# One more buffer for dK, paid for by a shared ring, in a fused two-block attention backward

## The chip, the cores and the metric

The kernel runs on one core of one Trainium2 chip. The metric is the device time of one execution in microseconds (us); less is better.

Engine names as in the profile: PE is TensorE's matmul, PEld its weight load, ACT is ScalarE, DVE is VectorE, POOL is GpSimd, SP is SyncE, whose queue issues the transfers.

## The reference

Two blocks A and B of multi-head attention over a given cache, forward and backward, all in bfloat16. Cut to what matters:

```python
# B=8, Sq=96, D=640, H=32, Sk=512, Dh=128, for block A and for block B
q = (x @ wq).reshape(B, Sq, H, Dh).transpose(0, 2, 1, 3)
p = softmax(einsum("bhqd,bhkd->bhqk", q, k_cache) * Dh ** -0.5)
o = einsum("bhqk,bhkd->bhqd", p, v_cache)
out = o.transpose(0, 2, 1, 3).reshape(B, Sq, H * Dh) @ wo
# result: concat([out_A, out_B], -1), and by jax.vjp the gradients
# dx, dk_cache, dv_cache, dwq, dwo of both blocks for a given grad_out
```

The gradients of the caches are as large as the caches: each of K, V, dK and dV is 8 x 32 x 512 x 128 elements per block, 33.6 MB. So a large part of the work is moving data.

## The kernel before

The kernel walks through block A, then block B, in pairs of heads (`HP = 2`) and, within a pair of heads, over the 8 batches. One (pair of heads, batch) is called a pair here and counted from 0, 128 in each block; pair 128 is the first of block B. A list of functions with a time tick and a slot is sorted and run once; this fixes the order in which each engine gets its instructions. A tick is one (head, batch), so a pair is two ticks. `OFF` says at which tick, relative to the pair, each stage stands:

```python
OFF = dict(kt=-3, vt=2, vn=1, kn=4, dv=7, dk=10, s2=3, s3=3, s4=4, s5=5, s6=6, s7=8, s8=9)
# kt: K transposed by the DMA   vt: V transposed by the DMA   vn, kn: V, K as they are
# dv, dk: stores of the gradients       s2...s8: the compute stages
```

Each pair has six transfers of 256 KB. All go through SyncE, and `sp` ties them into one fixed order: KT, V, store of dV, VT, K, store of dK.

```python
    def p_ldT(h, b, which):            # KT_p, VT_p: DMA transposes
            t_ = kvp.tile([128, F4 * KC, 16], BF16, name=key + "_p", bufs=5 if which == 0 else 4)
            sp(nc.sync.dma_start_transpose(t_[:], src))
# ... (cut)
    def p_ldn(h, b, which):            # K_sb, V_sb: plain loads
            t_ = kvp.tile([128, HP, KC, 128], BF16, name=key, bufs=4)
            sp(nc.sync.dma_start(t_[:].rearrange("p h c d -> p h (c d)"), src.rearrange("h (p c) d -> p h (c d)", c=KC)))
# ... (cut)
    def p_st(h, b, which):             # stores of dV_sb, dK_sb
            sp(nc.sync.dma_start(dst.rearrange("h (p c) d -> p h (c d)", c=KC), t_[:]))
```

`bufs=n` makes a ring of n tiles under one name: the next tile is to be had when the oldest of the n is no longer in use. A store that waits for its tile, or a load that waits for a free buffer, holds all that stand behind it on SyncE. The stages that the argument touches:

```python
    def c_s7(h, b):                    # dK of one head, written by ACT into half a tile
            for c in range(KC):
                nc.tensor.matmul(dK_ps[:, c * 128:(c + 1) * 128], dS_sb[:, c * 128:(c + 1) * 128], ...)
            if j == 0:
                st["dK_p"] = wk.tile([128, HP, KC * 128], BF16, name="dK_sb", bufs=3)
            nc.scalar.activation(dK_p[:, j], dK_ps[:], ACT.Identity, scale=1.0)
# ... (cut)
    # who reads the loads on PE:  V_sb in c_s45 (optp_ps), VT_p in c_s6 (dP_ps), K_sb in c_s78 (dq_dst_ps)
# ... (cut)
    def pA_wq(h):                      # wq of two heads
            wq_p = hd.tile([128, DC, HP * 128], BF16, name="wq_p", bufs=2)
    def qD(h, c_lo, c_hi):             # dwq of two heads, the same shape
                pr["dwq_sb"] = hd.tile([128, DC, HP * 128], BF16, name="dwq_sb", bufs=1)
    def qB(h, di):                     # dwo of one head goes through the ring "ob"
                st["dwo_sb"] = wk.tile([128, D], BF16, name="ob", bufs=4)
    def setup_stage(t):                # grad_out of block B, staged in the same ring "ob"
            S[("g_nat", t)] = wk.tile([128, D], BF16, name="ob", bufs=4)
# ... (cut)
            em.add(c0t + max(hk["qB"]) + 2, SL_LOAD + 0.3, qB_st(h))     # the store of dwo
```

Of the kernel before, what the change touches and what calls it, by code (L numbers as in the profile page):

```python
# [11 lines left out]
BF16 = mybir.dt.bfloat16  # L12
# [18 lines left out]
SL_LOAD = 0  # L31
# [13 lines left out]
HP = 2  # L45
# [32 lines left out]
def build_block(tc, em, tick0, blk, x, kc, vc, wq, wo, g_all, out_all, dx, dk, dv, dwq, dwo, ident, ones, pools, HG=4, first=True, groups=None):  # L78
    nc = tc.nc
    B, Sq, D = x.shape  # L80
    _, H, Sk, Dh = kc.shape
# [4 lines left out]
    DC = D // 128  # L86
    KC = Sk // 128
# [28 lines left out]
    const, ps, kvp, wk, hd, hst, grp = (pools[k] for k in ("const", "ps", "kvp", "wk", "hd", "hst", "grp"))  # L116

    def bank(shape, dt, name):
        return ps.tile(shape, dt, name=name, tag="bank")
# [48 lines left out]
    def evac(eng, dst, src, sc=None):  # L168
        if eng == "act":
            nc.scalar.activation(dst, src, ACT.Identity, scale=(1.0 if sc is None else sc))  # L170
        else:
            if sc is None:
                nc.vector.tensor_copy(dst, src)
            else:
                nc.vector.tensor_scalar(dst, src, float(sc), None, op0=ALU.mult)
# [19 lines left out]
    def pA_wq(h):  # L195
        def f():
            wq_p = hd.tile([128, DC, HP * 128], BF16, name="wq_p", bufs=2)
            with nc.allow_non_contiguous_dma(reason="per-pair wq slice"):
                sp(nc.sync.dma_start(wq_p[:], wq_v[:, :, h * 128:(h + HP) * 128]))
            for j in range(HP):  # L200
                HS[(blk, h + j)] = dict(wq_h=wq_p[:, :, j * 128:(j + 1) * 128])
        return f

    def pA(h):
        def f():
            g, hh = h // HG, h % HG
            if hh == 0:
                G[g] = dict(wo_r=grp.tile([128, HG, D], BF16, name="wo_r", bufs=2))
            wo_h = G[g]["wo_r"][:, hh]
            sp(nc.sync.dma_start(wo_h, wo[h * 128:(h + 1) * 128, :]))  # L210
            HS[(blk, h)]["wo_h"] = wo_h
            st = HS[(blk, h)]
        return f
# [86 lines left out]
    def h_alloc(h):  # L300
        def f():
            st = HS[(blk, h)]
            st["OT_h"] = hst.tile([128, T], BF16, name="OT_h", bufs=6)
            st["dQT_h"] = hst.tile([128, T], BF16, name="dQT_h")
        return f
# [140 lines left out]
    def c_s7(h, b):  # L446
        def f():
            st = CS[(blk, h, b)]
            hs = HS[(blk, h)]
            dS_sb = st["dS_sb"]  # L450
            dK_ps = bank([128, KC * 128], F32, "dK_ps")
            for c in range(KC):
                nc.tensor.matmul(dK_ps[:, c * 128:(c + 1) * 128], dS_sb[:, c * 128:(c + 1) * 128], hs["Qnat_h"][:, b * 128:(b + 1) * 128], start=True, stop=True)  # L453
            j = h % HP
            if j == 0:
                st["dK_p"] = wk.tile([128, HP, KC * 128], BF16, name="dK_sb", bufs=3)
            dK_p = CS[(blk, h - j, b)]["dK_p"]
            nc.scalar.activation(dK_p[:, j], dK_ps[:], ACT.Identity, scale=1.0)  # L458
        return f
# [35 lines left out]
    def qB_st(h):  # L495
        def f():
            sp(nc.sync.dma_start(dwo[h * 128:(h + 1) * 128, :], HS[(blk, h)]["dwo_sb"][:]))
        return f

    def qD(h, c_lo, c_hi):  # L500
        def f():
            pr = HS[(blk, h)]
            dQnat = pr["dQnat"]
            if "dwq_sb" not in pr:
                pr["dwq_sb"] = hd.tile([128, DC, HP * 128], BF16, name="dwq_sb", bufs=1)
            n = c_hi - c_lo
            w_ps = bank([128, 2, HP * 128], F32, "dwq_ps")
            for ci in range(n):
                c = c_lo + ci
                for t in range(TT):  # L510
                    nc.tensor.matmul(w_ps[:, ci, :], S["x_nat"][:, t, c * 128:(c + 1) * 128], dQnat[:, t, :], start=(t == 0), stop=(t == TT - 1))  # L511
            evac(EV["qD"], pr["dwq_sb"][:, c_lo:c_hi, :], w_ps[:, 0:n, :])
        return f
# [44 lines left out]
    for g in range(NG):  # L558
        h0 = GH0[g]
        for hh in range(groups[g]):  # L560
            h = h0 + hh
            j = h % HP
            c0t = tick0 + (h - j) * B
            hk = (HKE if first and h >= H - HP else HK if h >= HP else HK1 if first else HK2)[j]
            early = first and h < HP
            soon = 2 if first and HP <= h < 2 * HP and j == 0 else 0
            if j == 0:
                em.add(tick0 - 15 if early else c0t + hk["pA"] + soon, SL_LOAD + (1 if early else 0), pA_wq(h))
            em.add(tick0 + GT0 if early else c0t + hk["pA"] + soon, SL_LOAD - 1 if early else SL_LOAD, pA(h))
            em.add(c0t + hk["pB"], SL_HEAD, pB(h))  # L570
            em.add(c0t + OFF["s5"], SL_LOAD, h_alloc(h))
            for si in range(NTS):
                em.add(c0t + hk["pC0"][min(si, len(hk["pC0"]) - 1)], SL_HEAD, pC(h, 0, si))
                em.add(c0t + hk["pC1"][min(si, len(hk["pC1"]) - 1)], SL_HEAD, pC(h, 1, si))
            em.add(c0t + hk["pD1"], SL_HEAD, pD(h, 1))
            em.add(c0t + hk["pD0"], SL_HEAD, pD(h, 0))
            for b in range(B):
                ct = c0t + b * HP + j
                if j == 0:
                    em.add(tick0 - 13 if early and b == 0 else ct + (max(OFF["kt"], -1) if early else OFF["kt"]), SLOTS["LOAD"], p_ldT(h, b, 0))  # L580
                    em.add(ct + OFF["vt"], SLOTS["LOAD"], p_ldT(h, b, 1))
                    em.add(ct + OFF["vn"], SLOTS["LOAD"] + 0.1, p_ldn(h, b, 1))
                    em.add(ct + OFF["kn"], SLOTS["LOAD"] + 0.1, p_ldn(h, b, 0))
                    em.add(ct + OFF["dv"], SLOTS["LOAD"] + 0.2, p_st(h, b, 1))
                    em.add(ct + OFF["dk"], SLOTS["LOAD"] + 0.2, p_st(h, b, 0))
                em.add(ct + OFF["s2"], SLOTS["S2A"], c_s2a(h, b))
                em.add(ct + OFF["s2"], SLOTS["S2B"], c_s2b(h, b))
                em.add(ct + OFF["s3"], SLOTS["S3A"], c_s3a(h, b))
                em.add(ct + OFF["s3"], SLOTS["S3B"], c_s3b(h, b))
                em.add(ct + OFF["s5"], SLOTS["S5B"], c_s5b(h, b))  # L590
                em.add(ct + OFF["s4"], SLOTS["S4"], c_s4(h, b))
                S45.setdefault(ct + OFF["s5"], [None, None, None])[0] = (blk, h, b)
                S45.setdefault(ct + OFF["s4"], [None, None, None])[1] = (blk, h, b)
                S45.setdefault(ct + OFF["s6"], [None, None, None])[2] = (blk, h, b)
                S78.setdefault(ct + OFF["s8"], [None, None])[0] = (blk, h, b)
                S78.setdefault(ct + OFF["s7"], [None, None])[1] = (blk, h, b)
                em.add(ct + OFF["s6"], SLOTS["S6"], c_s6(h, b))
                em.add(ct + OFF["s7"], SLOTS["S7"], c_s7(h, b))
            em.add(c0t + hk["qA0"], SL_HEAD, qA(h, 0))
            for di in range(len(dsplits)):  # L600
                em.add(c0t + hk["qB"][min(di, len(hk["qB"]) - 1)], SL_HEAD + 1, qB(h, di))
            em.add(c0t + max(hk["qB"]) + 2, SL_LOAD + 0.3, qB_st(h))
            em.add(c0t + hk["qA1"], SL_HEAD, qA(h, 1))
            if j == HP - 1:
                for (k_, c_lo, c_hi) in hk["qD"]:
                    em.add(c0t + k_, SL_HEAD + 2, qD(h - j, c_lo, min(c_hi, DC)))
                em.add(c0t + k_ + 2, SL_LOAD + 0.3, qD_st(h - j))
        cLg = tick0 + (h0 + groups[g]) * B - 1
        gs0 = max(3, (GSPREAD0 * groups[g]) // HG)
        gs1 = max(3, (GSPREAD1 * groups[g]) // HG)  # L610
        em.add(cLg + OFF["s5"] - 2, SL_LOAD, gW(g))
        subs = [(t, di) for t in range(TT) for di in range(len(dsplits))]
        n = len(subs)
        for which in (0, 1):
            for i, (t, di) in enumerate(subs):
                if which == 0:
                    tk = cLg + OFF["s5"] + 2 + (i * gs0) // n
                else:
                    tk = cLg + OFF["s8"] + 2 + gs0 - 3 + (i * gs1) // n
                em.add(tk, SL_GRP, gU(g, which, t, di))  # L620
                if g == NG - 1 and di == len(dsplits) - 1:
                    em.add(tk + 2, SL_LOAD + 0.3, gU_st(g, which, t))
# [124 lines left out]
```

## Time and profile before

| | |
|---|---|
| time, median of 3 runs (lowest to highest) | 1650.46 us (1649.55 to 1652.88) |
| the execution that was profiled | 1642.09 us, its span 1640.3 |
| PE busy in it | 1602.0 us |
| moved by the DMA engines | 458 MB, 279 GB/s on average |

The profiled execution was 8 us shorter than the median.

The profile is read in four steps, whose lines the prediction shows: the page, for the engine that is busy nearly all the time; the table of waits, where a row says which engine and tile waited, for what, how long in total, how often, and at most; the timeline of PE, where the bracket at the end of a line is the idle time before it and what ended it; and the table of windows, for the clock (a "half-clock stretch" is one in which the granted clock was 0.50). A load that landed so many us before PE first used it has so many us "in hand".

Two more lines of the page say how large the thing is that the change is about. The first is a group of instructions (busy us, mean ns of one, then idle time before them and what ended most of it). The second is a kind of transfer (count, size, median us from issue to landing):

```profile
L458 ACT ACTIVATE dK_sb<-dK_ps 128x512 bf16<-128x512 f32 x512 | 305.4, 597 | 149.6 <-PE dK_ps L453 130.9
...
out_dram<-dK_sb SPq DMA_DIRECT2D x256, 256.0 KB, 4.5
```

ACT is idle for 149.6 us ahead of its 512 writes of dK, but nearly all of it (130.9) because the data is not there yet. Only 10.6 us are waits for a buffer.

### The profile page before, as it was taken

How to read it: one execution, taken by the hardware profiler on the slowest of the kernel's cores; microseconds unless marked ns; L12 is line 12 of the kernel's file. 1: busy time of each engine (PE TensorE's matmuls, PEld its weight loads, DVE VectorE, ACT ScalarE, POOL GpSimd, SP SyncE). 2: the span in 40 equal slices, each digit the busy share in tenths (PEclk: the TensorE clock that was granted, in tenths of full speed). 3: DMA queues.
4: the chain of work that ended last, by engine and by line, in shares of the span. 5: the costliest groups of instructions: out<-in, count | busy, mean ns of one | idle time of the engine just before them, and what ended most of it. 6: DMA issues, size and time to landing. Idle time of an engine off the chain costs nothing.

```text
span 1640.3 us, 55387 instructions
## 1 busy us (share of the span) xinstructions
PE 1602.0 (98%) x20713; PEld 1262.0 (77%) x20906; DVE 1340.0 (82%) x3406; ACT 1346.9 (82%) x3498; POOL 532.3 (32%) x1026
## 2 busy tenths in 40 slices
PE   8899999999999999999999999999999999999998
PEld 6777877878777787777777778777787777877776
DVE  5876888888888888878778778888888888888796
ACT  7889988879788788877868889788788888889783
POOL 1333333333333333333323333333333333333331
PEclk9999999999999999999999999999999999999999
DMA  9999999999999999999999999999999999999995
GB/s 263 261 293 273 292 291 282 275 275 279 276 292 289 290 280 282 280 276 258 284 289 311 289 288 273 290 290 283 275 287 278 272 290 287 281 292 285 284 267 167
DMA packets 375566, 458.12 MB, mean 279 GB/s; under 512 B 40704, under 2 KB 367104, under 8 KB 367104
## 3 DMA queue, kind: packets, MB, share of 16 engines
q1 hardware_dynamic: 375296, 454.57, 103.2%
q8 instruction: 163, 2.67, 0.7%
q14 instruction: 107, 0.88, 0.1%
HBM read 160.10 MB, written 159.12 MB: 195 GB/s over the span
## 4 chain that ended last, share of the span: by engine, by line
PE 89%; DMA 4%; ACT 4%; issue 2%; DVE 1%; SPq 0%; POOL 0%; ACTq 0%; DVEq 0%
PE o_ps L536 12%; PE q_ps L250 12%; PE dwq_ps L511 6%; PE dK_ps L453 6%; PE dV_ps L387 6%; PE S_ps L314 6%; PE dwo_ps L491 6%; PE dP_ps L411 6%; PE optp_ps L362 5%; PE optp_ps L369 5%; PE dq_dst_ps L430 5%; PE dq_dst_ps L437 5%; PE n_ps L265 3%; PE nat_ps L477 2%; DMA out_dram<-dK_sb 2%
## 5 line engine op out<-in xcount | busy, mean ns | idle before, releaser
L401 POOL TENSOR_TENSOR prod<-OT_h,dOT_h 128x96 bf16<-128x96 bf16 x512 | 187.1, 365 | 824.4 <-DVE rinv L336 438.2
L346 POOL TENSOR_SCALAR P_sb<-E_sb,rinv 96x512 bf16<-96x512 bf16 x508 | 349.8, 689 | 252.5 <-DVE rinv L336 252.1
L458 ACT ACTIVATE dK_sb<-dK_ps 128x512 bf16<-128x512 f32 x512 | 305.4, 597 | 149.6 <-PE dK_ps L453 130.9
L326 ACT ACTIVATE E_sb<-S_ps,negm 96x512 bf16<-96x512 f32 x512 | 350.9, 685 | 65.1 <-DVE negm L316 51.8
L316 DVE TENSOR_REDUCE negm<-S_ps 96x1 f32<-96x512 f32 x512 | 347.6, 679 | 67.2 <-PE S_ps L314 66.5
L415 DVE SCALAR_TENSOR_TENSOR dS_sb<-dP_ps,dl_ps,P_sb 96x512 bf16<-96x512 f32 x512 | 380.6, 743 | 1.6 <-PE optp_ps L369 1.4
L392 ACT ACTIVATE dV_sb<-dV_ps 128x512 bf16<-128x512 f32 x512 | 307.2, 600 | 3.9 <-PE dV_ps L387 2.6
L376 ACT ACTIVATE PT_sb<-optp_ps 128x384 bf16<-128x384 bf16 x512 | 255.2, 499 | 1.7 <-PE optp_ps L369 0.8
L439 DVE COPY dST_sb<-dq_dst_ps 128x384 bf16<-128x384 bf16 x512 | 177.5, 347 | 53.1 <-PE dq_dst_ps L437 51.5
L387 PE MATMUL dV_ps<-dOnat_h,P_sb 96*128 96x128 bf16 x2048 | 199.7, 219 | 2.1 <-DVE ob L546 1.0
L453 PE MATMUL dK_ps<-Qnat_h,dS_sb 96*128 96x128 bf16 x2048 | 198.9, 219 | 0.1
L411 PE MATMUL dP_ps<-VT_p,dOT_h 128*96 128x512 bf16 x512 | 195.8, 382 | 0.0
L314 PE MATMUL S_ps<-KT_p,QT_h 128*96 128x512 bf16 x512 | 194.0, 379 | 0.5 <-ACT E_sb L326 0.2
L453 PEld LDWEIGHTS <-dS_sb 96*128 96x128 bf16 x2048 | 147.5, 97 | 48.3 <-issue 0.6
L430 PE MATMUL dq_dst_ps<-dST_sb,K_sb 128*128 128x96 bf16 x2048 | 171.8, 205 | 3.0 <-ACT dK_sb L458 2.8
L369 PE MATMUL optp_ps<-ident,P_sb 96*128 96x96 bf16 x2048 | 172.4, 206 | 2.2 <-DVE P_sb L346 1.6
L362 PE MATMUL optp_ps<-PT_sb,V_sb 128*128 128x96 bf16 x2048 | 169.6, 204 | 3.0 <-ACT PT_sb L376 0.9
L437 PE MATMUL dq_dst_ps<-ident,dS_sb 96*128 96x96 bf16 x2048 | 171.8, 205 | 0.0
L536 PE MATMUL o_ps<-wo_r,OT_h 128*128 128x128 bf16 (+1 forms) x722 | 144.5, 294 | 2.4
L536 PE MATMUL o_ps<-wqT_h,dQT_h 128*128 128x512 bf16 (+1 forms) x720 | 144.2, 294 | 2.5
L362 PEld LDWEIGHTS <-V_sb 128*128 128x128 bf16 x2048 | 107.6, 96 | 50.7 <-issue 3.4
L491 PE MATMUL dwo_ps<-g_nat,Onat 128*128 128x128 bf16 (+1 forms) x735 | 129.4, 297 | 4.3 <-ACT dK_sb L458 2.6
(75 smaller groups left out, 3044.7 us busy)
## 6 DMA issues: line engine op xcount, KB each, us to landing
out_dram<-dV_sb SPq DMA_DIRECT2D x256, 256.0 KB, 4.4
out_dram<-dK_sb SPq DMA_DIRECT2D x256, 256.0 KB, 4.5
V_sb<-in_A_v_cache_dram SPq DMA_DIRECT2D x128, 256.0 KB, 4.3
K_sb<-in_A_k_cache_dram SPq DMA_DIRECT2D x128, 256.0 KB, 4.4
V_sb<-in_B_v_cache_dram SPq DMA_DIRECT2D x128, 256.0 KB, 4.3
K_sb<-in_B_k_cache_dram SPq DMA_DIRECT2D x128, 256.0 KB, 4.3
out_dram<-ob SPq DMA_DIRECT2D x88, 160.0 KB, 4.1
out_dram<-dwq_sb SPq DMA_DIRECT2D x32, 320.0 KB, 4.9
```

Source lines behind the costliest of these rows:

```text
L314: nc.tensor.matmul(S_ps[:], hs["QT_h"][:, tok], st["KT"], start=True, stop=True)
L316: nc.vector.tensor_reduce(negm[:], S_ps[:], axis=AX.X, op=ALU.max, negate=True)
L326: nc.scalar.activation(E_sb[:].rearrange("q (a f) -> q a f", f=F4), st["S_ps"][:].rearrange("q (f a) -> q a f", f=F4), ACT.Exp, bias=st["n ...
L346: eng.tensor_scalar(P_sb[:], st["E_sb"][:], st["rinv"][:], 0.0, op0=ALU.mult, op1=ALU.add)
L362: nc.tensor.matmul(OT_ps, st["V_sb"][:, c, :], st["PT_sb"][:, c * Sq:(c + 1) * Sq], start=(c == 0), stop=(c == KC - 1))
L387: nc.tensor.matmul(dV_ps[:, c * 128:(c + 1) * 128], P_sb[:, c * 128:(c + 1) * 128], hs["dOnat_h"][:, b * 128:(b + 1) * 128], start=True, s ...
L392: nc.scalar.activation(dV_p[:, j], dV_ps[:], ACT.Identity, scale=1.0)
L411: nc.tensor.matmul(dP_ps[:], hs["dOT_h"][:, tok], st["VT"], start=True, stop=True)
L415: nc.vector.scalar_tensor_tensor(dS_sb[:].rearrange("q (a f) -> q a f", f=F4), dP_ps[:].rearrange("q (f a) -> q a f", f=F4), dl_ps[:, 0:1] ...
L453: nc.tensor.matmul(dK_ps[:, c * 128:(c + 1) * 128], dS_sb[:, c * 128:(c + 1) * 128], hs["Qnat_h"][:, b * 128:(b + 1) * 128], start=True, s ...
L458: nc.scalar.activation(dK_p[:, j], dK_ps[:], ACT.Identity, scale=1.0)
L536: nc.tensor.matmul(o_ps[:], src[:, t * 128:(t + 1) * 128], rhs, start=(hh == 0), stop=(hh == groups[g] - 1))
```

## The change

dK tiles wait to be stored; a fourth tile gives the stores more time. Its 2048 bytes a partition have to come from somewhere: the dwq tile of 2560 bytes is given up, and dwq takes a slot of the ring of wq, which has the same shape. And near the boundary of the blocks, where both the dwo stores and the staged grad_out tiles want the four-slot ring `ob`, the dwo stores of six heads go out one tick sooner. The whole diff:

```diff
@@ -453,7 +453,7 @@
             if j == 0:
-                st["dK_p"] = wk.tile([128, HP, KC * 128], BF16, name="dK_sb", bufs=3)
+                st["dK_p"] = wk.tile([128, HP, KC * 128], BF16, name="dK_sb", bufs=4)
@@ -502,7 +502,7 @@
             if "dwq_sb" not in pr:
-                pr["dwq_sb"] = hd.tile([128, DC, HP * 128], BF16, name="dwq_sb", bufs=1)
+                pr["dwq_sb"] = hd.tile([128, DC, HP * 128], BF16, name="wq_p", bufs=2)
@@ -599,7 +599,7 @@
-            em.add(c0t + max(hk["qB"]) + 2, SL_LOAD + 0.3, qB_st(h))
+            em.add(c0t + max(hk["qB"]) + (1 if first and h >= H - 3 * HP else 2), SL_LOAD + 0.3, qB_st(h))
```

The built programs have the same instructions in the same order on PE, ACT and GpSimd; on SyncE six stores move.

## The prediction

> **What bounds the kernel now.** I read the page first: engines, slices, the chain that ended last.
>
> ```profile
> span 1640.3 us, 55387 instructions
> PE 1602.0 (98%) x20713; PEld 1262.0 (77%) x20906; DVE 1340.0 (82%) x3406; ACT 1346.9 (82%) x3498; POOL 532.3 (32%) x1026
> ...
> DMA  9999999999999999999999999999999999999995
> ...
> PE 89%; DMA 4%; ACT 4%; issue 2%; DVE 1%; SPq 0%; POOL 0%; ACTq 0%; DVEq 0%
> ```
>
> TensorE (PE) is busy 1602.0 of 1640.3 us, so all its idle time is 38.3 us, 2.3% of the span. The DMA row is at 9 in every slice but the last, so transfers are a close second limit. No change of buffers can win more than part of those 38.3 us, plus what slow clock stands behind them. So next I read the table of waits, for those that end on a buffer whose store has not landed, and what PE waited for behind them:
>
> ```profile
> ACT dK_sb L458 <- DMA out_dram<-dK_sb: 10.6, 6, 2.8
> ...
> ACT ob L170 <- DMA out_dram<-ob: 3.7, 1, 3.7
> ...
> PEld L159 <- DMA ob<-in_grad_out_dram: 3.1, 1, 3.1
> ...
> PE tp_ps L159 <- ACT ob L170: 2.9, 1, 2.9
> PE dq_dst_ps L430 <- ACT dK_sb L458: 2.8, 1, 2.8
> ...
> PE dwo_ps L491 <- ACT dK_sb L458: 2.6, 2, 1.7
> ...
> PE woT_ps L220 <- ACT dK_sb L458: 1.8, 1, 1.8
> ```
>
> Columns: us in total, times, longest. The reader sees the path: a dK store lands late, ScalarE (ACT) cannot write the next dK tile, and PE waits for a PSUM bank that ACT should have emptied. Over all rows PE waits 2.8+2.6+1.8+1.1+0.7+0.2 = 9.2 us for ACT's dK copy and 2.9 us for its `ob` copy. There is no row in which anything waits for the dwq tile or its store.
>
> Third, the timeline of PE and its weight loads at each stall. They lie in three places: 60 to 110 us (start of block A), 776 to 794 us (boundary), 880 to 920 us (soon after it).
>
> ```profile
> 70.62 0.10 PEld L430 LDWEIGHTS <-K_sb 128*128 128x128 bf16 x1 [1.64 <-DMA K_sb<-in_A_k_cache_dram]
> ...
> 71.97 0.33 PE L430 MATMUL dq_dst_ps<-dST_sb,K_sb 128*128 128x96 bf16 x4 [2.81 <-ACT dK_sb L458]
> ...
> 73.06 0.50 PE L362 MATMUL optp_ps<-PT_sb,V_sb 128*128 128x96 bf16 x4 [0.37 <-DMA V_sb<-in_A_v_cache_dram]
> ...
> 106.70 0.38 PE L491 MATMUL dwo_ps<-g_nat,Onat 128*128 128x512 bf16 x1 [0.90 <-ACT dK_sb L458]
> ...
> 793.92 0.44 PE L220 MATMUL woT_ps<-ident,wo_r 128*128 128x128 bf16 x5 [1.79 <-ACT dK_sb L458]
> ...
> 896.50 0.34 PE L362 MATMUL optp_ps<-PT_sb,V_sb 128*128 128x96 bf16 x4 [0.48 <-DMA V_sb<-in_B_v_cache_dram]
> ...
> 918.41 0.38 PE L491 MATMUL dwo_ps<-g_nat,Onat 128*128 128x512 bf16 x1 [1.69 <-ACT dK_sb L458]
> ```
>
> The dK waits do not stand alone: just behind two of them PE waits for a V_sb load. Fourth, the table of windows around the stall at 918 us, for the clock (columns: window, length, busy of PE, PEld, DVE, ACT, POOL, granted clock, DMA share, GB/s):
>
> ```profile
> 915.00:918.40 3.40, 1.73 (x29) 1.40 (x27) 2.33 (x6) 1.48 (x4) 1.40 (x3) 1.00 1.03 220
> 918.40:921.90 3.50, 3.44 (x19) 2.08 (x20) 0.75 (x2) 3.28 (x9) 0.69 (x1) 0.61 1.22 402
> ```
>
> After the stall the clock is 0.61, and PE gets 19 matmuls through in 3.5 us. The trace has three such half-clock stretches of 3.4 us in the body: from 72.7, 779.2 and 919.2 us.
>
> **What the Trainium skill says.** "Perfetto Trace Analysis", section Optimization Strategy: the same gap repeating "can mean there isn't enough SBUF/PSUM for the next tile to be allocated". The trace half agrees: the dK gaps are of that kind, but six short ones in 256 pairs of heads are not a steady bubble. "DMA: Bandwidth & Descriptors", section Anatomy of one DMA: about 2.0 us fixed plus bytes at 436 GB/s, an estimate of 2.6 us for the 256 KB store. The page's median for dK is 4.5 us from issue to landing and the shortest 2.1, so stores queue here for about 2 us. The same section says that DMA engines do not wait on semaphores, the issuing sequencer does. This fits SyncE's in-order queue, where dK stores leave 9 to 12 us after ACT finished the tile in the bad stretches, against a median of 5.5 over the run. "TensorE: Matmul & The Clock Gate", section What's actually happening: a free-running window of 3413 ns decides on 1.2 or 2.4 GHz. The trace agrees: stretches of 3.41 us at 0.50, each after a poorly filled 3.4 us. So a stall of 2 to 3 us can cost 3.41 x 0.5 = 1.7 us more.
>
> **The change part by part.** A comparison of the two built programs shows the same instructions in the same order on PE, ACT and GpSimd, a renamed tile on VectorE, and six moved stores on SyncE. So no engine work is added or removed, only waits.
>
> 1. *dwq into the wq ring.* This frees 5 x 256 x 2 = 2560 bytes a partition. A dwq tile of pair p is first written at step +37 of its pair, that is +5 of pair p+2. The wq tile whose slot it takes is that of pair p+2 (seen in the placement), last read at +1 of that pair, 4 steps earlier. The next wq load into the slot stands at +20 of pair p+2, 11 steps after the dwq store at +9. A step takes about 1640/512 = 3.2 us, so the store has some 35 us to land and needs 4.9 (median). Cost 0, gain 0.
>
> 2. *Fourth dK buffer*, 2 x 512 x 2 = 2048 bytes, paid for by part 1. A store now has 2 steps, 6.4 us, more to land, and the longest wait was 2.8. All six waits should go. What PE wins depends on the next wait, stall by stall, from landings in the trace:
>  - 69 to 72 us: K_sb landed at 70.6 and V_sb at 73.0, so PE stands at 73.06 again. 0.
>  - 106 us: the V_sb loads of the next pairs have 1.5 us or more in hand. Gain 1.0, and about 0.4 for a small one at 89 us. Sum 1.4.
>  - 792 us: PE lost 1.95 us; the next V_sb load has only 1.7 us in hand. Gain 1.6.
>  - 886 and 900 us: PE lost 0.7 and 0.5, but the V_sb loads of pairs 138 to 143 landed 0.0 to 0.5 us before use. The twelve g_nat and x_nat loads from 854 us on fill the queue (302 GB/s from 870 to 930 us against 279 on average). Gain 0.3.
>  - 918 us: PE lost 1.85 plus 1.7 of half clock = 3.5; the next V_sb load has 2.76 us in hand. Gain 2.5.
>  Sum 1.4+1.6+0.3+2.5 = 5.8 us.
>
> 3. *dwo stores one step sooner*, heads 26 to 31 of block A. The ACT copy at 778.90 waited for head 27's store, issued at 773.20 and landed at 778.82, though the tile was full at 758. Its new place is behind the dV store of 768.49, 4.2 us sooner, so ACT's 3.7 us go. None of the six tiles is still being filled at its new place, so SyncE does not stop there. But PE's transposes at 779.23 also needed the staged grad_out tile, issued at 773.75 and landed at 779.18. One issue fewer ahead of it helps 0.5 us, which comes off the same 1.7 to 2.2 us that the V_sb loads have in hand at the boundary. Gain 0.3.
>
> Total 5.8+0.3 = 6.1, say 6 us: 1650.46 - 6 = 1644.5 us.
>
> **The rivals.**
> - *The wait moves to the loads.* PE waits for V_sb and K_sb instead, as SyncE's queue and the DMA engines set the pace in the bad stretches. For: V_sb just in time at 73, 103 and 883 to 914 us, DMA share at or over 1.0. Against: at 106, 792 and 918 us loads have 1.5 to 2.8 us in hand. Taken wholly it leaves 0 to 2 us: 1648.5 to 1650.5.
> - *All stalls go, and the slow clock with them.* 9.2 + 2.9 us of waits and three half-clock stretches, 3 x 1.7 = 5.1 us: 17.2 us, 1633 us. For: SyncE's longest issues end on PE by the table of waits, so a faster PE might also make loads leave sooner. Against: several of them end about 0.2 us after some earlier DMA landed, which looks like a full queue.
> - *The wq ring becomes the wait.* A wq load held by a dwq store would stop SyncE's whole in-order queue, tens of times: some us per pair, 1660 or more. For: the dwq store is 320 KB and lands slowly. Against: the 35 us above.
> - *The sooner dwo stores stop SyncE* until ACT has filled them. Against: the tiles were full 2 us or more before. It would cost 1 to 3 us.
>
> **Range and chances.** I take the middle of the first two rivals, nearer the first: 1644.5 us, range 1638.5 to 1649.5. The runs of before spread over 3.3 us, so the change may hardly show. A gain of 2% is 33 us, about twice what all these waits and slow clocks hold, so 1% for faster. Slower by 2% would need the third rival: 1%. Within 2%: 98%.
>
> **What would show it right or wrong.** Right: no row of ACT waiting for a dK store; PE still standing at about 73 us and between 883 and 914 us, with V_sb or K_sb loads named; the half-clock stretch at 919 us gone; PE's busy time within 1% of 1602, idle time from 38 to about 32 us; the `ob` wait of ACT gone while the transposes near 779 us still wait for the staged tile. Wrong: a wait on wq_p beyond the kernel's start; idle time of PE below 28 us (then the loads followed PE, and the second rival holds); a dK wait that stays (then the queue lags by more than 6 us). If the stretch from 880 to 920 us shrinks by more than 4 us, my reading that loads set its pace is wrong.

## The result, and the profile after

| | median us | lowest to highest | runs |
|---|---|---|---|
| before | 1651.56 | 1649.55 to 1652.88 | 6 |
| after | 1647.75 | 1642.39 to 1652.04 | 6 |

The ratio of after to before is 0.9976, with a 95% interval of 0.9954 to 0.9998. Ratios here are the mean time of one kernel's fast runs over that of the other's of the same rounds, so not quite the ratio of the medians that stand in the tables. The change is worth some 4 us, and 1647.75 lies inside the predicted range.

The page of after: span and engines, and the chain of work that ended last, as shares of the span.

```profile
span 1644.9 us, 55391 instructions
...
PE 1600.7 (97%) x20713; PEld 1260.4 (77%) x20906; DVE 1340.4 (81%) x3406; ACT 1349.3 (82%) x3498; POOL 533.3 (32%) x1026
...
PE 88%; DMA 6%; ACT 2%; DVE 2%; issue 1%; POOL 0%; SPq 0%; DVEq 0%; ACTq 0%
```

PE's busy time is the same. In the chain, ACT fell from 4% to 2% and DMA rose from 4% to 6%: what ACT's writes no longer cost, transfers now seem to cost. (The exchange is better read from the waits below: ring_only and dwo_only, two longer executions with three dK buffers, have DMA at 6% too.) But this execution is *longer* than the profiled one of before (1640.3), though the kernel is a little faster over all runs. Two single executions cannot settle a difference of 4 us here; I come back to it.

The table of waits of after, rows of PE (us in total, times, longest):

```profile
PE optp_ps L362 <- DMA V_sb<-in_A_v_cache_dram: 5.8, 6, 2.0
...
PE dP_ps L411 <- DMA VT_p<-in_A_v_cache_dram: 3.9, 2, 2.3
...
PE optp_ps L362 <- DMA V_sb<-in_B_v_cache_dram: 3.0, 5, 1.0
...
PE dP_ps L411 <- DMA VT_p<-in_B_v_cache_dram: 2.3, 1, 2.3
...
PE tp_ps L159 <- DMA ob<-in_grad_out_dram: 2.2, 1, 2.2
```

No row of ACT waiting for a dK store is left, and none of ACT waiting for `ob`. In their place PE itself waits for loads: 5.8 + 3.9 + 3.0 + 2.3, and 0.6 for K_sb, are 15.6 us, where in the profile of before the same sum is 1.3. The timeline of PE shows where (start, length, instruction, and in brackets the idle time before it and what ended it):

```profile
69.62 0.42 PE L411 MATMUL dP_ps<-VT_p,dOT_h 128*96 128x512 bf16 x1 [2.28 <-DMA VT_p<-in_A_v_cache_dram]
...
71.66 0.34 PE L430 MATMUL dq_dst_ps<-dST_sb,K_sb 128*128 128x96 bf16 x4 [0.59 <-DMA K_sb<-in_A_k_cache_dram]
...
74.08 0.50 PE L362 MATMUL optp_ps<-PT_sb,V_sb 128*128 128x96 bf16 x4 [1.41 <-DMA V_sb<-in_A_v_cache_dram]
...
123.80 0.34 PE L362 MATMUL optp_ps<-PT_sb,V_sb 128*128 128x96 bf16 x4 [1.61 <-DMA V_sb<-in_A_v_cache_dram]
...
312.18 0.34 PE L362 MATMUL optp_ps<-PT_sb,V_sb 128*128 128x96 bf16 x4 [2.01 <-DMA V_sb<-in_A_v_cache_dram]
...
783.62 1.33 PE L159 MATMUL tp_ps<-ident,ob 128*128 128x128 bf16 x15 [2.18 <-DMA ob<-in_grad_out_dram]
...
796.30 0.42 PE L411 MATMUL dP_ps<-VT_p,dOT_h 128*96 128x512 bf16 x1 [1.61 <-DMA VT_p<-in_A_v_cache_dram]
...
923.73 0.42 PE L411 MATMUL dP_ps<-VT_p,dOT_h 128*96 128x512 bf16 x1 [2.29 <-DMA VT_p<-in_B_v_cache_dram]
```

The stalls stand where they stood (about 70, 780 to 796, and 920 us), with another name at the end of the line. At 106 us PE no longer stalls. The stalls at 124 us and at 312 us, in the middle of block A, are new.

The table of windows of after at the stall of 923 us (window, length, busy of PE, PEld, DVE, ACT, POOL, granted clock, DMA share, GB/s):

```profile
920.30:923.70 3.40, 1.14 (x20) 0.97 (x18) 1.76 (x6) 2.23 (x7) 1.04 (x2) 1.00 1.16 227
923.70:927.20 3.50, 3.42 (x42) 2.48 (x44) 1.96 (x7) 2.19 (x6) 1.04 (x2) 1.00 0.72 234
```

In the profile of before PE was busy for 1.73 of 3.40 us ahead of the matmul at 918.41, and the next 3.5 us ran at 0.61. Here it was busy for only 1.14 of 3.40 us, and the clock stayed at 1.00. The half-clock stretches at 779 and 919 us are both gone; the one at 72 us is 6.8 us long instead of 3.4.

One more measure, from when each load landed and when PE first used it. A dK tile lay free for 5.08 us (median) before ACT wrote into it, at least 0.08, and for 9.88 us, at least 3.82, in after. So about 5 us of slack went to the stores. A V_sb load lay ready for 6.32 us (median) in before and for 4.84 us in after; those with under 0.5 us in hand went from 9 to 23. That the loads lost these 1.5 us to the stores is not shown: ring_only and dwo_only (both below), with three dK buffers but in longer executions than that of before, have 5.12 and 5.05 us, with 17 and 24 loads under 0.5.

### The profile page after: what moved, and what is told of

Same layout as the page of the kernel before. It is cut to its first block, busy times and chain, and to the rows that moved or that the text cites. A ratio compares the mean times of both kernels' runs of the same rounds, so it can differ in the third digit from the quotient of the medians.

```text
span 1644.9 us, 55391 instructions
## 1 busy us (share of the span) xinstructions
PE 1600.7 (97%) x20713; PEld 1260.4 (77%) x20906; DVE 1340.4 (81%) x3406; ACT 1349.3 (82%) x3498; POOL 533.3 (32%) x1026
## 4 chain that ended last, share of the span: by engine, by line
PE 88%; DMA 6%; ACT 2%; DVE 2%; issue 1%; POOL 0%; SPq 0%; DVEq 0%; ACTq 0%
PE o_ps L536 12%; PE q_ps L250 12%; PE dwq_ps L511 6%; PE dV_ps L387 6%; PE dK_ps L453 6%; PE S_ps L314 6%; PE dwo_ps L491 6%; PE dP_ps L411 6%; PE optp_ps L362 6%; PE optp_ps L369 5%; PE dq_dst_ps L430 5%; PE dq_dst_ps L437 5%; PE n_ps L265 3%; PE nat_ps L477 3%; DMA V_sb<-in_A_v_cache_dram 2%; DMA V_sb<-in_B_v_cache_dram 1%
## 5 line engine op out<-in xcount | busy, mean ns | idle before, releaser
L316 DVE TENSOR_REDUCE negm<-S_ps 96x1 f32<-96x512 f32 x512 | 347.5, 679 | 67.9 <-PE S_ps L314 67.2
L362 PE MATMUL optp_ps<-PT_sb,V_sb 128*128 128x96 bf16 x2048 | 169.6, 204 | 10.2 <-DMA V_sb<-in_A_v_cache_dram 5.8
L373 DVE CAST OT_h<-optp_ps 128x96 bf16<-128x96 f32 x512 | 125.0, 244 | 10.9 <-PE optp_ps L369 10.0
```

The source lines that it names most:

```text
L316: nc.vector.tensor_reduce(negm[:], S_ps[:], axis=AX.X, op=ALU.max, negate=True)
L362: nc.tensor.matmul(OT_ps, st["V_sb"][:, c, :], st["PT_sb"][:, c * Sq:(c + 1) * Sq], start=(c == 0), stop=(c == KC - 1))
```

## The experiments

The theory at this point: the fourth buffer took the waits for dK away, and most of what it won was given back to the loads, because SyncE's order and the DMA engines set the pace in the bad stretches. Rivals: the gain comes from another part of the change (the ring, the sooner stores); or what loads wait for is only the order of SyncE, or only the number of bytes.

A yardstick for all runs: the time from the first use of V_sb in one pair to that in another. In the middles of the blocks a pair takes 6.2 us (622.1 / 100 and 649.8 / 104). The other stretches hold more or less of the work that comes once in several pairs, so a pair there takes 5.6, 6.8 and 6.2 us in before: compare the numbers of one column with each other. One profiled execution each, us:

| kernel | pairs 3 to 16 | 20 to 120 | 118 to 132 | 134 to 146 | 146 to 250 |
|---|---|---|---|---|---|
| before | 73.0 | 622.1 | 95.6 | 73.8 | 649.8 |
| before_again | 71.1 | 622.2 | 95.0 | 72.9 | 649.8 |
| after | 72.9 | 625.4 | 94.5 | 73.8 | 649.8 |
| after_again | 73.2 | 628.6 | 98.3 | 73.9 | 649.7 |
| dk4_only | 73.2 | 631.2 | 95.8 | 73.5 | 649.8 |
| ring_only | 72.7 | 627.7 | 97.3 | 73.0 | 649.7 |
| dwo_only | 75.9 | 628.9 | 94.9 | 74.9 | 649.7 |
| skip8 | 72.7 | 627.1 | 95.8 | 67.6 | 649.8 |
| v_on_pool | 67.9 | 631.8 | 90.7 | 71.0 | 659.3 |
| loads_sooner | 77.5 | 679.7 | 109.9 | 83.7 | 705.2 |
| mix | 69.1 | 622.8 | 99.7 | 71.9 | 650.0 |
| mix_dk3 | 70.8 | 623.0 | 95.6 | 77.0 | 649.7 |
| extras_pool | 73.1 | 623.3 | 92.0 | 74.1 | 650.7 |
| vk_sooner | 73.3 | 632.0 | 97.7 | 70.3 | 651.6 |

The middle of block B is the same to 0.1 us in all kernels that leave the loads alone. The middle of block A is not: 622 to 631 us, and most of the difference in length between the profiled executions lies there. The traces show what fills it: from the first use of V_sb in pair 20 to that in pair 120, PE waits for no load and behind no dK copy in before and before_again (622.1 and 622.2 us), and for 2.3 to 6.3 us in after, ring_only, dwo_only, after_again and dk4_only (625.4 to 631.2 us): for loads with four buffers, for loads and behind dK with three.

All times in one table (us; each batch shares one chip and its runs of before; the four chips are different ones, and before differs by 7 us between them, so only ratios are compared across batches):

| batch | kernel | median | lowest to highest | before, median | ratio | 95% interval |
|---|---|---|---|---|---|---|
| 1 | dk4_only | 1646.93 | 1641.46 to 1653.01 | 1650.66 | 0.9972 | 0.9943 to 1.0000 |
| 1 | dwo_only | 1647.93 | 1646.27 to 1652.59 | 1650.66 | 0.9988 | 0.9963 to 1.0012 |
| 1 | ring_only | 1647.86 | 1642.97 to 1653.00 | 1650.66 | 0.9984 | 0.9957 to 1.0012 |
| 1 | after_again | 1646.44 | 1636.03 to 1652.47 | 1650.66 | 0.9971 | 0.9935 to 1.0006 |
| 2 | before_again | 1642.54 | 1641.20 to 1642.85 | 1644.44 | 0.9993 | 0.9967 to 1.0018 |
| 2 | v_on_pool | 1651.41 | 1647.35 to 1655.80 | 1644.44 | 1.0053 | 1.0019 to 1.0087 |
| 2 | loads_sooner | 1806.86 | 1797.30 to 1819.54 | 1644.44 | 1.1001 | 1.0959 to 1.1043 |
| 2 | skip8 | 1635.88 | 1631.42 to 1641.92 | 1644.44 | 0.9956 | 0.9926 to 0.9986 |
| 3 | mix | 1639.34 | 1633.71 to 1643.82 | 1643.32 | 0.9972 | 0.9952 to 0.9992 |
| 3 | mix_dk3 | 1641.00 | 1635.86 to 1643.22 | 1643.32 | 0.9976 | 0.9959 to 0.9993 |
| 3 | extras_pool | 1642.63 | 1641.18 to 1650.17 | 1643.32 | 1.0001 | 0.9983 to 1.0020 |
| 4 | vk_sooner | 1646.11 | 1639.45 to 1652.88 | 1650.09 | 0.9960 | 0.9935 to 0.9984 |

All results were correct, but for skip8.

### The parts one by one: dk4_only, dwo_only, ring_only, after_again

dk4_only is the changed kernel with the stores of dwo at their old place:

```diff
-            em.add(c0t + max(hk["qB"]) + (1 if first and h >= H - 3 * HP else 2), SL_LOAD + 0.3, qB_st(h))
+            em.add(c0t + max(hk["qB"]) + 2, SL_LOAD + 0.3, qB_st(h))
```

> The change without the sooner dwo stores (ring shared, dK in four buffers). Theory A (the prediction's sum: the fourth dK buffer carries the gain, 5.8 of 6.1 us): 3 to 6 us under the kernel before, within 1 us of the whole change; in the trace no wait of ACT for a dK store, and V_sb or VT_p waits of PE of 8 us or more in sum, where before had under 2. Rival B (the sooner dwo stores carry it): within 1 us of before. In both the ACT wait of 3 to 4 us for a dwo store near 778 us is back.

dwo_only is the kernel before with that one line of the change.

> The kernel before with only the dwo stores sooner. Theory A: within 1 us of before (0.3 us gain); the dK waits stay at about 10 us in sum; ACT's wait for a dwo store near 778 us is gone, but PE's transposes there still wait 2 to 3 us, now for the staged grad_out tile alone. Rival B: 3 us or more under before and the transposes no longer wait.

ring_only is the kernel before with dwq in the ring of wq, and nothing else.

> The kernel before with only the dwq tiles in the wq ring (dK still three buffers). All theories of the ring costing nothing: within 1 us of before, and no wait on wq_p outside the first 10 us. Rival C (a hidden cost of the ring that eats part of the gain of the dK buffer): 2 us or more over before, with SyncE's wq load or VectorE's dwq copy waiting for each other.

after_again is the changed kernel once more, beside the others on the same chip.

> The whole change once more, so that its parts are compared on one chip: 2 to 6 us under before (it was 0.9976 of before); the sum of the three parts' differences should match it within 2 us.

Measured: 0.9972, 0.9988, 0.9984 and 0.9971. The two with four dK buffers are at 4 to 5 us, the two with three at 2 to 3. Each interval is 5 to 7 thousandths wide, so no pair of these can be told apart by time. Two expectations for dwo_only were missed: its dK waits were 23.0 us and not about 10, and its transposes waited 0.6 us for grad_out's tile and not 2 to 3. A second run of the kernel before under its own name tells what such a ratio is worth:

> The kernel before once more, for a second profile and for the noise between equal kernels. Its first profile was an execution of 1642 us, while its median is 1651. Theory A (transfers late in single executions make the scatter): an execution near 1650 us shows more than the six dK waits of the first profile, 12 or more and over 15 us in sum, and the head pairs 20 to 120 of block A take longer than the 622 us of the first profile, while pairs 146 to 250 stay at 649.7. Rival B (a lower clock or slower matmuls): the same waits as before, all stretches longer alike. Time ratio 1.000 within its interval.

It measured 0.9993. (Its profiled execution took 1642.37 us, on a chip whose runs of before had a median of 1644.44: a short one again, with 10.2 us of dK waits, so the part of the expectation that asked for a long execution was not met. The long executions with three buffers that it asked for are ring_only and dwo_only: 16 dK waits each, and 627.7 and 628.9 us for pairs 20 to 120.)

The waits tell more than the times. In batch 1 all profiled executions were long ones (spans of 1648 to 1651 us). Rows of the waits of dwo_only:

```profile
ACT dK_sb L458 <- DMA out_dram<-dK_sb: 23.0, 16, 3.0
```

of ring_only:

```profile
ACT dK_sb L458 <- DMA out_dram<-dK_sb: 21.5, 16, 2.8
...
ACT ob L170 <- DMA out_dram<-ob: 3.8, 1, 3.8
```

and of dk4_only:

```profile
PE optp_ps L362 <- DMA V_sb<-in_A_v_cache_dram: 7.0, 11, 1.2
...
ACT ob L170 <- DMA out_dram<-ob: 3.5, 1, 3.5
```

First: dK waits are 21 to 23 us in a long execution with three buffers, against 10 in a short one, and gone with four, whatever else is changed. Second: the wait of ACT for `ob` goes with the old place of the dwo stores. It is there in before, ring_only and dk4_only (3.7, 3.8, 3.5), for no known reason not in before_again, and in none of dwo_only, after and after_again. Third, and this is the main finding, add up all rows of PE that end on a load of K or V, and all that end on ACT's dK copy:

| profiled execution | span | PE waits for K and V loads | PE waits behind dK | both |
|---|---|---|---|---|
| before | 1640.3 | 1.3 | 9.2 | 10.5 |
| before_again | 1640.6 | 1.7 | 7.6 | 9.3 |
| ring_only | 1649.5 | 2.7 | 12.2 | 14.9 |
| dwo_only | 1648.4 | 6.4 | 13.6 | 20.0 |
| dk4_only | 1651.2 | 18.3 | 0.6 | 18.9 |
| after | 1644.9 | 15.6 | 0.0 | 15.6 |
| after_again | 1650.7 | 17.5 | 0.3 | 17.8 |

The fourth buffer turns waits behind dK into waits for loads, about one for one: among the long executions, ring_only and dwo_only against dk4_only and after_again, 12 to 13 us behind dK went and 11 to 16 for loads came. What is left of a gain does not show in a single execution: the sum of both is no smaller with four buffers.

### What the loads wait for: skip8, v_on_pool, extras_pool

skip8 leaves out eight dV stores of 256 KB in the bad stretch of block B, so one gradient is wrong there:

```diff
-                    em.add(ct + OFF["dv"], SLOTS["LOAD"] + 0.2, p_st(h, b, 1))
+                    if first or not (6 <= h // HP * B + b < 14):
+                        em.add(ct + OFF["dv"], SLOTS["LOAD"] + 0.2, p_st(h, b, 1))
```

> Wrong result on purpose: the whole change without the eight dV stores of pairs 134 to 141 (block B, 2 MB), to take transfers out of the bad stretch from 870 to 925 us. Theory E: the waits of PE for V_sb and VT_p between 880 and 930 us (7 us in the profile of the whole change) fall under 2 us, and pairs 134 to 146 take 67 us or less instead of 73.8. Rival (that stretch is bound by something else, the extra PE work or ACT): it stays above 72 us.

The stretch of pairs 134 to 146 falls from 73.8 to 67.6 us, just short of the 67 expected, and no load wait of over 0.5 us is left between 880 and 930 us. The table of windows of after, then that of skip8, for the same 40 us:

```profile
880.00:920.00 40.00, 35.91 (x481) 27.82 (x483) 31.76 (x81) 34.33 (x89) 13.47 (x26) 1.00 1.07 304
```

```profile
880.00:920.00 40.00, 39.27 (x546) 31.18 (x543) 35.28 (x90) 37.29 (x101) 14.72 (x29) 1.00 1.04 274
```

PE is busy for 39.27 instead of 35.91 us, with 274 instead of 304 GB/s moved. An estimate: 8 x 262144 bytes are 2.1 MB, and at 304 GB/s that is 6.9 us; 6.2 were won. So this stretch is set by transfers. What skip8 does not tell is whether by their bytes, by SyncE's having fewer to issue, or by its not having to wait for the eight dV tiles.

extras_pool moves the additional loads that fill that stretch (g_nat, x_nat of block B, and the wo loads) from SyncE to GpSimd's queue. The bytes stay, though not their times, as the trace shows.

```diff
-            sp(nc.sync.dma_start(S[key][:, t0_:t1_, :], ...))
+            put = (lambda *a: sp(nc.sync.dma_start(*a))) if first else nc.gpsimd.dma_start
+            put(S[key][:, t0_:t1_, :], ...)
# the wo loads likewise, except those of the first two heads
```

> The whole change, with other issues taken off SyncE instead: the 12 reloads of g_nat and x_nat for block B and the wo loads go to GpSimd's queue, so the copies between the transposes stay in SyncE. If the number of SyncE issues in the stretch of 854 to 925 us is what makes it lag, pairs 134 to 146 take 70 us or less instead of 73.8. If it is the bytes on the 16 DMA engines, it stays above 72.5. Pairs 3 to 16 have few such loads: 72 to 73 us either way. Time 1 to 5 us under the whole change in the first case.

The stretch stays at 74.1 us, and the whole at 1.0001. Fewer issues on SyncE did not help there. But GpSimd is not bound to SyncE's order: it issued the twelve g_nat and x_nat loads between 844.7 and 860.4 us, all landed by 867.7, where SyncE in after issued them from 860.3 to 907.7. PE then stood for 2.1 us in all at three loads between 870 and 878 us, and for 3.2 us at a KT_p load at 884 us, and was busy for all 20 us from 885 to 905. So the run moved the loads in time as well. With skip8 it leans to the bytes, as the waits came right behind the burst; it does not prove it.

v_on_pool moves all V_sb loads to GpSimd's queue, with the same bytes:

```diff
-            sp(nc.sync.dma_start(t_[:]..., src...))
+            if which == 1:
+                nc.gpsimd.dma_start(t_[:]..., src...)
+            else:
+                sp(nc.sync.dma_start(t_[:]..., src...))
```

> The whole change, with the natural V_sb loads issued by GpSimd on its own queue instead of in SyncE's in-order queue. Theory Q (the order and lag of SyncE's queue hold the V_sb loads back, the 16 DMA engines have room): the V_sb and VT_p waits of PE fall from about 15 us to under 4, and the time falls by 8 us or more under before. Theory E (the DMA engines themselves are full in the bad stretches): V_sb waits may go, but VT_p, K_sb or KT_p waits of about the same sum take their place, and the time stays within 5 us of the whole change; it may be over it, if descriptors made by GpSimd are slower.

Here the start of block A answers: pairs 3 to 16 take 67.9 us instead of 73. The windows of after, then of v_on_pool:

```profile
40.00:110.00 70.00, 64.30 (x877) 52.38 (x881) 56.05 (x144) 62.51 (x168) 25.70 (x51) 0.95 1.06 264
```

```profile
40.00:110.00 70.00, 67.71 (x951) 54.86 (x949) 60.04 (x155) 66.45 (x180) 37.96 (x67) 1.00 1.04 289
```

289 instead of 264 GB/s, with the same transfers: in this stretch the bytes were not the whole limit, SyncE's single order was part of it. The Trainium skill, "DMA: Bandwidth & Descriptors", section Issuing engines are not separate DMA queues, says that issuing from more engines only saves the sequencer's issue time, as all run on the same 16 DMA engines. The trace agrees for pairs 134 to 146, where little is won (71.0 us instead of 73.8), and at the start of block A it shows that taking the loads out of SyncE's queue can be worth 5 us; whether by the issue time saved or by the loads' no longer waiting behind others in SyncE's order, this run does not separate. PE's waits for V_sb and VT_p fell to 4.6 us, where under 4 were expected. Yet the kernel as a whole is slower, 1.0053. The lines of V's loads among the groups of instructions of v_on_pool, and a row of its waits, say why:

```profile
L289 POOL DMA_DIRECT2D V_sb<-in_A_v_cache_dram x128 | 96.4, 753 | 151.1 <-PE optp_ps L372 143.2 <-DVE rinv L339 3.6 <-DVE Qnat_h L173 2.1
```

```profile
PE dl_ps L416 <- POOL prod L404: 14.4, 26, 0.8
```

GpSimd works 753 ns for each issue, 193 us for all 256, and waits in between for PE, probably for a buffer to come free (143.2 us in block A). `prod`, which it also makes, comes later, and PE waits for that: 14.4 us. The middles of both blocks are 10 us longer than in before.

### Only where it is needed: mix, mix_dk3

mix moves V's loads to GpSimd's queue only at the two starts of blocks and at the end of block A, with four dK buffers; mix_dk3 is the same with three.

```diff
-            sp(nc.sync.dma_start(t_[:]..., src...))
+            pool_q = which == 1 and (h < 6 or (first and h >= H - 4))
+            put = nc.gpsimd.dma_start if pool_q else lambda *a: sp(nc.sync.dma_start(*a))
+            put(t_[:]..., src...)
```

> The whole change, with the V_sb loads on GpSimd's queue in the bad stretches alone (heads 0 to 5 of each block and the last four of block A). With every V_sb load there, the stretches of pairs 3 to 16, 118 to 132 and 134 to 146 took 67.9, 90.7 and 71.0 us against 73, 95 to 98 and 73.8, but the pairs in the middle got slower by about 10 us in each block. If the lag of SyncE's queue holds the loads back and the loss lies in the middle, this keeps the gain of about 10 us and not the loss: 0.993 of before or less, and it beats the whole change. If the gain was only chance of one execution: within 3 us of the whole change.

> The same with three dK buffers. If the dK wait and the V_sb wait lie in series (taking one away shows the other), then the fourth dK buffer is worth more here than in the kernel before: this is 5 us or more slower than mix, and ACT waits for dK stores more often than the 7 times of before, with PE behind it. If the dK wait only appears because SyncE's queue lags, taking the V_sb issues out of it cures both: within 2 us of mix, dK waits under 5 us in sum.

Both gained the same, 0.9972 and 0.9976. The 0.993 hoped for from mix was missed, and so was the loss of 5 us of mix_dk3 against mix; of its other theory the time held (within 2 us of mix), but not the dK waits of under 5 us. A row of the waits of mix_dk3, then two of mix:

```profile
ACT dK_sb L460 <- DMA out_dram<-dK_sb: 15.2, 10, 3.4
```

```profile
PE tp_ps L159 <- DMA ob<-in_grad_out_dram: 4.9, 4, 1.4
...
PE dP_ps L413 <- DMA VT_p<-in_B_v_cache_dram: 3.7, 3, 2.0
```

With three buffers the dK waits are back (15.2 us on ACT, 9.5 on PE behind it). With four they are gone, and PE waits 4.7 us for loads and 6.8 for grad_out's tile or behind `ob`, where mix_dk3 has 2.1 and none. It is the same exchange as before: 11.6 us with three buffers against 11.5 with four. Neither is told apart from the changed kernel by time.

### Loads sooner: loads_sooner, vk_sooner

If loads are what PE waits for, one could issue V, VT and K a tick sooner.

```diff
-OFF = dict(kt=-3, vt=2, vn=1, kn=4, dv=7, dk=10, ...)
+OFF = dict(kt=-3, vt=1, vn=0, kn=3, dv=7, dk=10, ...)
```

> The whole change, with V_sb, VT_p and K_sb loads one step sooner in the queue, so ahead of the stores of that step. Theory Q (order): loads gain up to 3 us in hand, waits of PE for V_sb and VT_p fall to under 5 us, 5 to 8 us under before beyond noise. Theory E (engines full): the order only shifts which transfer is late; waits for loads fall by less than half, dK or dV waits of ACT may appear, the time is within 3 us of the whole change.

It was 10% *slower*. Nothing in the theory explained that. The trace: the order on SyncE is now such that KT and VT, the two DMA transposes, are issued one right behind the other. VT comes first, KT right behind it. The times of SyncE's issue of KT and VT (minimum, median, maximum in ns; first and last start in us), in loads_sooner, then that of KT in after:

```profile
L277 SPq DMA_TRANSPOSE KT_p<-in_B_k_cache_dram x128: 1296/2155/4566, 871.0 to 1747.3; - x128
...
L277 SPq DMA_TRANSPOSE VT_p<-in_B_v_cache_dram x128: 1095/1168/3477, 882.5 to 1756.8; - x128
```

```profile
L277 SPq DMA_TRANSPOSE KT_p<-in_B_k_cache_dram x128: 1095/1184/2766, 798.9 to 1592.3; - x128
```

The second of two transposes in a row holds the queue for 2.16 us instead of 1.18; the first takes 1.17, where VT in after takes 1.38. Over the whole trace all issues of SyncE take 1616 us where those of after take 1456: 160 us more, and the kernel is 162 us slower than before (medians). All transfers behind come later: the rate falls from 288 to 259 GB/s (between 1300 and 1400 us), and stores of dV are now late as well, in a row of its waits:

```profile
ACT dV_sb L392 <- DMA out_dram<-dV_sb: 112.4, 90, 3.5
```

vk_sooner tests this: the same, but VT stays where it was, so that no two transposes are adjacent.

```diff
-OFF = dict(kt=-3, vt=2, vn=1, kn=4, dv=7, dk=10, ...)
+OFF = dict(kt=-3, vt=2, vn=0, kn=3, dv=7, dk=10, ...)
```

> The whole change with V_sb and K_sb loads one step sooner and VT_p where it was, so that SyncE's order is transpose, two copies, transpose, two copies again. In loads_sooner the VT_p and KT_p transposes stood next to each other, the second one's issue took 2.1 us at the median instead of 1.2, and the time rose 10%. If adjacent transposes were the cause (theory T): within 1% of before, KT_p issues back at 1.2 us median, and ACT's 112 us of waits for dV stores gone. If the sooner loads were the cause, by stopping SyncE on buffers that PE has not read yet (theory W): 5% or more over before, with V_sb and K_sb issues above 0.6 us at the median. If T holds and V_sb loads then have 3 us more in hand, the time is 3 to 6 us under the whole change; if the queue's rate sets the pace, it is equal within 3 us.

KT's issue is back at 1.19 us, and the 10% are gone: 0.9960.

```profile
L277 SPq DMA_TRANSPOSE KT_p<-in_B_k_cache_dram x128: 1095/1186/2851, 806.2 to 1600.3; - x128
```

ACT's waits for dV stores are gone too. So what cost 10% is VT's new place beside KT; that it is their being adjacent is read from the time of KT's issue. That VT, a tick sooner, had to wait for a buffer is not what the trace shows: its own issue became shorter. The ratio 0.9960 is the lowest of all correct kernels, but its interval overlaps that of the changed kernel. And the waits were exchanged once more, for V_sb now no waits to speak of, and for VT_p (in its waits):

```profile
PE dP_ps L411 <- DMA VT_p<-in_A_v_cache_dram: 18.6, 12, 4.1
```

No version that I ran beats both kernels beyond doubt.

## Why the prediction was right or wrong

The class and the range held: 1647.75 us in 1638.5 to 1649.5, "within 2%". The point, 1644.5, was 3.3 us too low: 4 us gained of the predicted 6. The range is a weak test: it is 11 us wide, and on two other chips the kernel before itself had medians inside it (1644.44 and 1643.32). And the sum behind the point did not come true, as its largest term won nothing in the profiles; that the number came near is in part luck. By its steps:

- **The dwq tile in the ring costs nothing, gains nothing: held.** After the start of the kernel nothing on PE, ACT or VectorE waits for a load of wq or a store of dwq in after (VectorE's 36.2 us ahead of its dwq copies are for data from PE, as 35.2 us were in before), and ring_only differs from before by less than its interval. The third rival is refuted.
- **All dK waits go: held,** in all nine profiled kernels with four buffers no row of ACT waiting for a dK store is left (10.6 us in the short execution of before; ring_only and dwo_only show 21 to 23 in long ones).
- **What PE wins behind them, stall by stall: nearly half of it failed, and more is in doubt.** At 72 us nothing was won, as said: PE stands at 74.08 for V_sb, and pairs 3 to 11 even take 45.5 us where they took 44.0. At 106 us the stall is gone, as said, and pairs 11 to 16 take 27.5 us where they took 29.0; but PE then stands for 1.61 us at 123.80, for V_sb, and pairs 16 to 20 take 29.4 us where they took 27.9. At 886 to 914 us V_sb loads hold PE (3.0 us in all), as said. The term that failed is the one at 918 us, 2.5, the largest of the sum. Pairs 134 to 146 took 73.8 us before and 73.8 after, where 0.3 + 2.5 were to go: PE now stands for 2.29 us at 923.73, for VT_p. The 1.6 of the boundary are in doubt: PE stands for 1.61 at 796.30, for VT_p again, where it lost 1.79 at 793.92; pairs 118 to 132 went from 95.6 to 94.5 in after, but to 98.3 in after_again. The step that failed is "the next V_sb load has 2.76 us in hand": it looked at V_sb and not at the transpose. The load that holds PE at 923.73 is VT_p of pair 143, which had only 0.43 us in hand in before. It held PE in all three profiles of four buffers with the six transfers of each pair unchanged: 2.29 us in after, 1.81 in after_again (at 929.60) and 2.12 in dk4_only (at 930.10); and pairs 134 to 146 took 73.5 to 73.9 us in them, and 72.9 to 74.9 in the four kernels with three buffers and SyncE loads. Loads of VT_p with less than 0.5 us in hand went from 3 to 9 (6 and 8 in ring_only and dwo_only).
- **The clock: half right.** The half-clock stretches at 779 and 919 us went, as said, but not because PE no longer stalls, and it proves nothing for the change: ring_only and dwo_only, with three buffers, have none at 919 us either, and after_again and dk4_only have one at 788 and 789. Four stalls of over 2 us in after (69.6, 312, 783 and 923 us) were followed by a single half-clock stretch, of 6.8 us, from 72 us on; the windows behind the other three show 1.00. A stall *can* cost 1.7 us more, but whether it does is not to be had from its length. Nor does the busy share of the 3.41 us before it tell: in before_again PE was busy for 1.90 us from 915.47 us on and half clock followed, in dwo_only for 1.76 us from 782.70 on and none followed.
- **The dwo stores: held in after.** ACT's wait for `ob` is gone in each kernel that has the line (but for 0.6 us in loads_sooner), the transposes still wait 2.18 us for the staged tile (0.6 in dwo_only), and nothing of it shows in the time (dwo_only, 0.9988).
- **The rivals.** The first, that the wait moves to the loads, is what the waits show: 15.6 to 18.3 us for loads instead of 8 to 14 behind dK. I gave it a 0 to 2 us gain and took a point nearer to it than to the second, and that was still too high; its own gain was too low, if the 4 us are real. The second (17 us) is refuted, and the fourth too: SyncE issues the six moved stores in 0.41 to 0.42 us each in after.
- **The checks: one was badly made.** PE's idle time was to fall from 38 to about 32 us; the profile of after shows 1644.9 - 1600.7 = 44.2. It proves nothing: the profiled executions differ by 10 us and more for the same kernel. Nor is 38 us all idle: both profiles have 20713 matmuls, those of the later runs 20906, as many as PEld has loads. 193 records are missing from the first two. In before_again, with all of them, PE is busy for 1614.1 of 1640.6 us, so some 26 us are idle in a short execution. The bound that the prediction set on any gain was 12 us too wide.

**Is the gain real?** Three comparisons of kernels that have the fourth buffer and SyncE loads gave 0.9976, 0.9972 and 0.9971. Each interval ends at 1.000 or just beside it. That they agree speaks for a gain of about 4 us over before. But ring_only and dwo_only, for which I expected next to nothing, gave 0.9984 and 0.9988 on the same chip. Against those the fourth buffer is worth about 2 us, which is less than these runs can tell apart.

**What stays open:** how the 4 us fall to the three parts, and what makes the middle of block A take 622 us in one execution and 631 in another of nearly the same program, while the same stretch of block B takes 649.8 always. That scatter is larger than the whole effect. It goes with PE's waits for late transfers there, with three buffers as with four; no run here tells why they are late.

## What to carry to other kernels

If a wait for a buffer is removed in a kernel whose transfers are nearly always busy, look at *every* load that is next in line, the transposed ones too, and credit only the smallest time in hand. Before trusting a single profile for a difference of a few us, check where its execution lies among the timed ones, and whether it holds all records. If loads are issued from one queue, reorder with care: two DMA transposes in a row cost this kernel 10%.

## What the Trainium skill lacked or had wrong

- "DMA: Bandwidth & Descriptors", section DMA Transpose (X-bar), has nothing on what it costs to issue one transpose right behind another in one queue; of order it has only that two streams must not transpose at once. Here the issue of the second took 2.16 us (median) instead of 1.18, and the kernel 1.1001 times as long.
- The same page, section Anatomy of one DMA: its fit gives 2.6 us for 256 KB, an estimate, for GpSimd's path; the prediction took it for SyncE's stores, for which the section has none. For SyncE's dK stores the page of the profile shows a median of 4.3 to 4.7 us in all kernels; the shortest took 2.15, so less than the fit. For them the fit tells neither the floor nor the time in a full queue.
- The same page, section Issuing engines are not separate DMA queues, calls the issue time saved usually small, and names no other gain. Moving all V loads to a second queue was worth 5 us of 73 at the start of block A (issue time and order not separated), and cost GpSimd 753 ns for each load, which the section does not weigh against it.
- "Perfetto Trace Analysis", section Optimization Strategy, says that a repeated gap can be a sign of too few buffers. The fourth buffer removed all waits for a dK buffer, and PE's waits for loads were 15.6 to 18.3 us, where three buffers had 1.3 to 6.4. The section has no word that, where stores and loads share a queue, waits for a buffer can come back as waits for loads.
- "TensorE: Matmul & The Clock Gate", section What's actually happening, was borne out in that the window is free-running: the three half-clock stretches of before start at 72.65, 779.21 and 919.15 us, 207.0 and 41.0 times 3.413 us apart. It gives no length of stall that is safe: one of 2.29 us did not bring the half clock at 923 us in after, one of 1.69 us did at 918 in before.
